# Expert 0's weights behind its gathers, and two experts in split fp32r products

## The chip, the cores and the metric

The kernel runs on one core of a Trainium2 chip. The metric is the device time of one execution in microseconds (us); of several executions the median is taken. A core has a matrix engine (TensorE, PE in the profile; its weight loads are PEld), VectorE (DVE), ScalarE (ACT), GpSimd (POOL) and SyncE (SP), which here only issues DMAs. Each works through its instructions in order. TensorE's granted clock has two levels, 2.4 GHz (1.00 in the rows) and 1.2 GHz (0.50).

## The reference

Three stages, one after the other. q, k and v have 4 batches, 12 heads, 448 positions and 64 values a head.

```python
scores = scale * np.matmul(q, k.transpose(0, 1, 3, 2))      # causal mask, softmax
attn_out = np.matmul(attn, v)                               # 1792 tokens of 768 values
logits = x @ w_gate                                         # 8 experts
# pairs (token, expert) in falling order of logit; a token goes to its best
# expert that has room; an expert takes 224 tokens
for e in range(E):
    h = np.maximum(x[mask] @ w1[e], 0.0)                    # 768 x 1024
    out[mask] = h @ w2[e]                                   # 1024 x 768
gate = 1.0 / (1.0 + np.exp(-(x @ w_gate2)))                 # 768 x 1536
return (gate * (x @ w_val) @ w_out).astype(np.float32)
```

The last stage's weights arrive in 64-bit floating point and are converted in the kernel.

## The kernel before, in words

**Attention** works in 24 units of two heads each (`prep`, `qk`, `exps`, `trans`, `av`). `prep` (L248) transposes q or k on TensorE, takes a high part `hi` in fp32r (a float format that TensorE multiplies in one pass) on ScalarE (L258) and the rest `lo` on VectorE (L270). GpSimd copies the high halves into `st` and `qz` (L263, L265), and SyncE brings the other halves to the opposite partitions by DMA (L267, L273). `qk` (L279) multiplies them, two products a head with 112 weight columns (L290, L291). Ahead of that, GpSimd sets up constants, fills the mask (L237), loads the gate weights `wr` (L240) and splits them into `wg` (L241, L242); `logits` (L373) uses `wg` one unit later.

**Routing** finds the tokens of an expert in a phase (`phase`, L515); phase 0 runs alone between attention and the experts. `search` (L474) finds a threshold in levels: compares on VectorE (L490), counts on TensorE (L495), a step back (L507), a new constant (L501). At the end a table of places `o1` (L608) and an operand `r4` (L601, L602) give, over 14 small products (L612), the token numbers `ids` (L615). SyncE stores them to `idx_d` (L617), 224 numbers of 4 bytes, which only the last stage reads. Two indirect DMAs of GpSimd (`gather`, L739) fetch the 224 token rows of 3 KB each from `x_d`. `xprep` (L744) transposes them (L752). The phases of experts 1 to 7 are spread between the products of the experts (`tick`, `step`): TensorE's order there is that of the program, and its routing products are put in after a count of estimated product times.

**The experts** (`moe`, L758) take one expert after the other, 4 chunks of w1 and 4 of w2, each 768 KB, loaded by SyncE in two halves (`load_chunk` L666, `load_half` L696). Chunks go by turns into buffers `wh` and `wl`, four each, so eight chunks can be ahead. Chunks 2 to 7 are put behind the store of the places of expert 0 in the order of issue (L674); no semaphore holds them. A product `mm` (L713) of an expert is in fp32: 96 products of 128 weight columns and 224 tokens, which the trace shows as 192 matmuls.

**moe2** (L804) is the last stage, in two halves of tokens. Its chunks are converted by `conv_half` and `conv_split` (L65 to L94) into high and low parts (buffers `wh` and `wl` again), and every product is three fp32r products of high and low parts. The first half converts and stores the parts to DRAM, the second reads them back.

A scheduler orders the instructions of all engines but TensorE by simulated times when the kernel is built; `issue_after` adds an order without a wait, `high_priority` moves instructions ahead, `add_manual_dep` adds a dependence that is waited for.

Of the kernel before, what the change touches and what calls it, by code (L numbers as in the profile page):

```python
# [7 lines left out]
F32 = mybir.dt.float32  # L8
# [22 lines left out]
def body(ctx: ExitStack, tc: tile.TileContext, q, k, v, moe_w_gate, moe_w1, moe_w2,  # L31
# [46 lines left out]
    def conv_split(cs, hn, ln):  # L78


        hw, lw = cs[:, :, 1], cs[:, :, 0]
        k3 = cv.tile([128, HC], U32, name="k3")
        nc.scalar.activation(k3, lw, AF.Copy, scale=2.0 ** -29)
        sq = cv.tile([128, HC], F32, name="sq")
# [21 lines left out]
    colp = ct([R, 128], BF, "colp")  # L106
    nc.gpsimd.iota(colp, pattern=[[1, 128]], base=0, channel_multiplier=0, allow_small_or_imprecise_dtypes=True)
# [129 lines left out]
    nc.gpsimd.memset(mask[:, :S - P], 0.0)  # L237
# [3 lines left out]
    nc.gpsimd.tensor_copy(wg[:, :, :E], wr)  # L241
    nc.gpsimd.tensor_tensor(wg[:, :, E:], wr, wg[:, :, :E].bitcast(F32), op=OP.subtract)  # L242
# [171 lines left out]
    for f in [prep(1, 0), prep(1, 1)]:  # L414
        f()
    for s in range(LA):
        qk(*steps[s])
# [49 lines left out]
    fins, after, ist = {}, {}, {}  # L467
# [6 lines left out]
    def search(key, half):  # L474
        base = cst = None
        for lv, (J, st_) in enumerate(LEVELS):
            s_ = st_ * (65536.0 if half == 0 else 1.0)
            thr = JC[half, st_]
            if lv:
                tt = rtile([R, 33], F32, "thr")  # L480
                V.tensor_scalar(tt[:, :J], thr, acc, cst, op0=OP.add, op1=OP.add)
                thr = tt[:, :J]
            ca = rps([R, 128])
            c, a = ca[:E, :64], ca[:, 64:]
            cmps = []
            for hf in range(2):
                ts = slice(hf * T // 2, (hf + 1) * T // 2)
                cmp = rtile([R, T // 2, 64], BF, "cmp", bufs=2)
                with tc.issue_after(after.pop("cmp")) if "cmp" in after else ExitStack():
                    V.tensor_tensor(cmp[:, :, :J], key[:, ts, None].to_broadcast([R, T // 2, J]),  # L490
                                    thr[:, None, :].to_broadcast([R, T // 2, J]), op=OP.is_ge)
# [12 lines left out]
            ge = rtile([E, 64], BF, "ge")  # L504
            V.tensor_scalar(ge[:, :K_], c[:, :K_], rem8, None, op0=OP.is_ge)
            yield Y[3]
            nc.tensor.matmul(a[:, :K_], STEP[half, st_], ge[:, :K_], start=True, stop=True)  # L507
            jk = rtile([R, 64], F32, "jk")
            acc = rtile([R, 1], F32, "acc", bufs=2)
            V.tensor_scalar(jk[:, :K_], a[:, :K_], s_, None, op0=OP.min, op1=OP.add, accum_out=acc)  # L510
        th = rtile([R, 1], F32, "th", bufs=2)
        V.tensor_tensor(th, acc, cst, op=OP.add)
        return th, thr, c

    def phase(ph):  # L515
# [101 lines left out]
        ist[ph] = nc.sync.dma_start(idx_d[ph * CAP:(ph + 1) * CAP].rearrange("(h p) o -> p (h o)", p=P), ids[ph])  # L617
# [48 lines left out]
    def load_chunk():  # L666
        kind, a, c = chunks[stream["next"]]
        if kind in ("w1", "w2") and a not in regs:
            regs[a] = nc.sync.value_load(ei[a][0:1, 0:1], min_val=0, max_val=E - 1)
        if kind in ("w1", "w2"):  # L670
# [25 lines left out]
    def load_half(kind, a, c, n, raw):  # L696
        if kind == "w1":
            src = moe_w1[bass.ds(regs[a], 1), n * 384:(n + 1) * 384, c * 256:(c + 1) * 256]
            nc.sync.dma_start(raw.rearrange("p (c f) -> p c f", c=3),
                              src.rearrange("a (c p) f -> p (a c) f", p=128))  # L700
        else:
# [3 lines left out]
            nc.sync.dma_start(raw.rearrange("p (c f) -> p c f", c=2),  # L705
                              src.rearrange("a (c p) f -> p (a c) f", p=128))
# [28 lines left out]
    def gather(ph):  # L735
        xs = []
        for h in range(2):
            xg = mo.tile([P, DM], F32, name="xg", bufs=2)
            nc.gpsimd.indirect_dma_start(out=xg, out_offset=None, in_=x_d[:],  # L739
                                         in_offset=bass.IndirectOffsetOnAxis(ap=ids[ph][:, h:h + 1], axis=0))  # L740
            xs.append(xg)
        XE[ph] = xs

    def xprep(ph):  # L744
        xs = XE[ph]
        xx = mo.tile([128, KD, CAP], F32, name="xx", bufs=2)
        for dp in range(3):
# [5 lines left out]
            nc.scalar.activation(xx[:, 2 * dp:2 * dp + 2], w.rearrange("p a h q -> p a (h q)"), AF.Copy)  # L753
        XE[ph] = xx
# [3 lines left out]
    def moe(ph, nxt):  # L758
        xx = XE[ph]
        hs_ = []  # L760
        for c in range(4):
            w = use(("w1", ph, c)).rearrange("p (c f) -> p c f", c=KD)
            if c % 2 == 0:
                hs_.append(mp.tile([128, 4, CAP], F32, name="hx", bufs=3))
            g = ps.tile([128, 512], F32, name="g", bufs=7)
            for f in range(2):
                for d in range(KD):
                    mm(g[:, f * CAP:(f + 1) * CAP], w[:, d, f * 128:(f + 1) * 128], xx[:, d], d == 0, d == KD - 1)
            hx = hs_[c // 2][:, 2 * (c % 2):2 * (c % 2) + 2]
            nc.scalar.activation(hx, g[:, :2 * CAP].rearrange("p (a t) -> p a t", a=2), AF.Relu)  # L770
# [8 lines left out]
        for dp in range(0, KD, 2):  # L779
# [4 lines left out]
            for f0, f1 in ((0, 6), (6, 8)) if dp == 0 else ((0, 8),):  # L784
                for n in range(2):
                    d = dp + n
                    for f in range(f0, f1):
                        a = ws[2 * (d // 3) + f // 4].rearrange("p (c f) -> p c f", c=4)
                        mm(yo[n], a[:, f % 4, (d % 3) * 128:(d % 3) * 128 + 128], hs_[f // 4][:, f % 4], f == 0, f == 7)
# [116 lines left out]
```

## Time and profile before

| | us |
|---|---|
| median of 3 runs | 1171.52 (1170.42 to 1171.89) |
| the profiled execution | 1172.35 |
| its span, from the first to the last instruction | 1170.6 |
| busy in it: PE, DVE, ACT, POOL | 1121.1, 595.0, 368.1, 118.3 |
| mean granted TensorE clock | 0.98 |

All rows come from the profiled execution; times in them are us from the start of its span. Durations of groups are means in ns where they stand after a comma. A bracket at the end of a timeline row is the idle time of the engine ahead of it and what ended it. "To landing" is the time from the issue of a DMA to the semaphore that tells of its end.

### The profile page before, as it was taken

The page shows a single profiled execution, that of the slowest core. Times are in us where ns is not written, and L with a number is a line of the kernel's source. Part 1 is how long each engine was busy: PE and PEld are TensorE (multiplying, and loading weights), DVE is VectorE, ACT ScalarE, POOL GpSimd, SP SyncE. Part 2 cuts the span into 40 slices and gives each one's busy share as a digit, 9 for nine tenths or more (in the row PEclk, how much of TensorE's full clock was granted, in tenths as well). Part 3 has the DMA queues.
Part 4 walks back from the last instruction along what each step waited for, and adds up shares of the span by engine and source line. Part 5 has one row for each costly group of instructions (what it writes and reads, how often), then busy time and mean ns, then how long its engine had stood idle before and what let it go on. Part 6 is the DMA issues. An engine that isn't in the chain of part 4 may idle for free.

```text
span 1170.6 us, 19295 instructions
## 1 busy us (share of the span) xinstructions
PE 1121.1 (96%) x7317; PEld 1047.0 (89%) x7317; DVE 595.0 (51%) x1855; ACT 368.1 (31%) x723; POOL 118.3 (10%) x231
## 2 busy tenths in 40 slices
PE   6999999962999999999999999999999999999997
PEld 5999999951888898899999999999999999999997
DVE  5777777763554455450028668688625103223223
ACT  4767676730011110121126544443312220100100
POOL 6333333200000000000000000000002000000002
PEclk9999999975999999999999999999999999999999
DMA  8555656336477665767569555565335333333302
GB/s 167 119 143 146 151 139 157 75 101 184 147 151 184 129 166 156 176 189 198 186 214 326 211 208 218 197 227 203 139 108 203 108 108 108 108 108 109 109 1 95
DMA packets 159581, 180.62 MB, mean 154 GB/s; under 512 B 74864, under 2 KB 140416, under 8 KB 159488
## 3 DMA queue, kind: packets, MB, share of 16 engines
q1 hardware_dynamic: 156064, 168.11, 47.1%
q0 software_dynamic: 2496, 11.04, 4.7%
q8 instruction: 58, 0.95, 0.3%
q14 instruction: 35, 0.29, 0.1%
q10 hardware_dynamic: 928, 0.23, 0.1%
HBM read 129.01 MB, written 39.33 MB: 144 GB/s over the span
## 4 chain that ended last, share of the span: by engine, by line
PE 93%; DMA 3%; DVE 2%; POOL 1%; issue 1%; POOLq 0%; SPq 0%
PE g L714 70%; PE o L343 8%; PE w L323 4%; PE s L290 2%; PE s L291 2%; DMA xg<-x_d,ids 2%; PE r L495 2%; PE w L252 1%; PE g L752 1%; PE w L381 1%; PE w L364 1%; PE r L507 0%; DMA wl<-in_moe_w_dram 0%; DMA wr<-in_moe_w_gate_dram 0%; POOL qz L233 0%
## 5 line engine op out<-in xcount | busy, mean ns | idle before, releaser
L714 PE MATMUL g<-x2h,wh 128*128 128x448 f32 x576 | 212.1, 368 | 0.0
L714 PE MATMUL g<-x2h,wl 128*128 128x448 f32 x576 | 212.0, 368 | 0.0
L714 PE MATMUL g<-x2l,wh 128*128 128x448 f32 x576 | 212.0, 368 | 0.0
L714 PE MATMUL g<-wh,hx 128*128 128x384 f32 x672 | 172.5, 334 | 0.0
L823 DVE TENSOR_TENSOR g<-g,gv 128x448 f32<-128x448 f32 x48 | 30.3, 632 | 219.2 <-PE g L714 219.1
L714 PEld LDWEIGHTS g<-wh,hx 128*128 128x128 f32 x672 | 121.5, 188 | 0.2
L714 PEld LDWEIGHTS g<-x2h,wl 128*128 128x128 f32 x576 | 108.1, 188 | 10.8
L714 PEld LDWEIGHTS g<-x2h,wh 128*128 128x128 f32 x576 | 108.1, 188 | 10.8
L714 PEld LDWEIGHTS g<-x2l,wh 128*128 128x128 f32 x576 | 108.1, 188 | 10.6
L714 PE MATMUL g<-wl,hx 128*128 128x384 f32 x336 | 112.2, 334 | 0.0
L343 PE MATMUL o<-vt,pt 112*112 112x65 f32 x960 | 106.4, 258 | 0.1
L343 PEld LDWEIGHTS o<-vt,pt 112*112 112x112 f32 x960 | 101.9, 178 | 0.3 <-DVE pt L312 0.3
L847 DVE TENSOR_TENSOR acc<-g,acc 128x384 f32<-128x384 f32 x140 | 75.8, 555 | 38.3 <-PE g L714 38.2
L301 ACT ACTIVATE sm<-sm,mn 112x112 f32<-112x112 f32 (+1 forms) x192 | 90.3, 522 | 6.5 <-DVE mn L293 6.5
L293 DVE CUSTOM_DVE_ANT_0 sm<-s,mask 112x112 f32<-112x112 f32 (+1 forms) x192 | 78.3, 444 | 24.3 <-PE s L291 24.1
L714 PE MATMUL g<-hx,wh 128*128 128x224 f32 x384 | 87.3, 361 | 0.0
L714 PE MATMUL g<-xx,wh 128*128 128x224 f32 x384 | 83.7, 364 | 0.0
L714 PE MATMUL g<-hx,wl 128*128 128x224 f32 x384 | 83.0, 356 | 0.0
L94 DVE TENSOR_TENSOR wl<-ca,wh 128x768 fp32r<-128x768 f32 x36 | 33.3, 955 | 91.9 <-PE g L714 81.9
L714 PE MATMUL g<-xx,wl 128*128 128x224 f32 x384 | 79.8, 357 | 0.0
L820 ACT ACTIVATE gv<-g 128x448 f32<-128x448 f32 x48 | 26.0, 542 | 168.0 <-PE g L714 168.0
L714 PEld LDWEIGHTS g<-xx,wh 128*128 128x128 f32 x384 | 71.5, 193 | 1.2
(188 smaller groups left out, 1621.5 us busy)
## 6 DMA issues: line engine op xcount, KB each, us to landing
wh<-in_moe_w_dram SPq DMA_DIRECT2D x64, 384.0 KB, 4.8
wl<-in_moe_w_dram SPq DMA_DIRECT2D x64, 384.0 KB, 5.6
wsc<-wh SPq DMA_DIRECT2D x18, 768.0 KB, 3.3
wsc<-wl SPq DMA_DIRECT2D x18, 768.0 KB, 4.4
wl<-wsc SPq DMA_DIRECT2D x36, 384.0 KB, 4.8
wh<-wsc SPq DMA_DIRECT2D x36, 384.0 KB, 4.4
cs<-in_moe_w_gate_dram SPq DMA_DIRECT2D x12, 768.0 KB, 5.0
cs<-in_moe_w_val_dram SPq DMA_DIRECT2D x12, 768.0 KB, 6.2
```

The source lines that it names most:

```text
L94: nc.vector.tensor_tensor(ln, w_, hn.bitcast(F32), op=OP.subtract)
L290: nc.tensor.matmul(ss[j], qq[:, j, qs], kh[:, j, :w], start=True, stop=False)
L291: nc.tensor.matmul(ss[j], QZ[u % NZ][:, j, qs], kl[:, :w], start=False, stop=True)
L293: nc.vector.tensor_tensor_reduce(sm[:, j, :w], ss[j], mask[:, S - w:], op0=OP.add, op1=OP.min, scale=1.0, scalar=3.0e38, accum_out=mn[:, j ...
L301: nc.scalar.activation(sm[:, j, :w], sm[:, j, :w], AF.Exp, bias=mn[:, j:j + 1], scale=-1.0)
L323: nc.tensor.transpose(w[:P, n, :], sm[:, j, c * P:(c + 1) * P], ident[:P, :P])
L343: nc.tensor.matmul(o[:, n, j, :], pt[:, j * (i + 1) + c, :], vt[:, j, c, :], start=c == 0, stop=c == i)
L495: nc.tensor.matmul(c[:, :J], oha[:, tt_, :], cmps[2 * tt_ // T][:, tt_ % (T // 2), :J], start=tt_ == 0, stop=tt_ == T - 1)
L714: nc.tensor.matmul(o, a, b, start=first, stop=last_)
L820: nc.scalar.activation(gv, pg[:, :448], AF.Sigmoid)
L823: nc.vector.tensor_tensor(pv[:, :448], pv[:, :448], gv, op=OP.mult)
L847: nc.vector.tensor_tensor(ac, po[:, :384], ac, op=OP.add)
```

## The change

- The split of the gate weights moves on GpSimd from ahead of the load of unit 1 to behind the casts of units 0 and 1; part of the mask is filled by VectorE in place of GpSimd.
- In `search`, the constant of a level is issued behind the compares of that level. `r4` is made ahead of the table `o1`; the table has 112 columns that are computed and 16 that are set to zero once.
- Chunks 2 to 7 (expert 0's later weights) wait for both gathers of expert 0, by a dependence that is waited for.
- Experts 6 and 7 compute each product as three fp32r products (high x high, high x low, low x high). Their weights are loaded into `raw` buffers (four halves); ScalarE makes the high part and VectorE the low part. Such a chunk takes a `wh` and a `wl` buffer, so four can be ahead. Token rows and hidden values get low parts too. `k3` and `sq` of the conversion have one buffer each in place of two.

```diff
+        k3 = cv.tile([128, HC], U32, name="k3", bufs=1)
+        sq = cv.tile([128, HC], F32, name="sq", bufs=1)
...
-    colp = ct([R, 128], BF, "colp")
+    colp = ct([R, P], BF, "colp")
+    o1 = ct([R, T, 128], BF, "o1")
...
-    nc.gpsimd.memset(mask[:, :S - P], 0.0)
+    nc.vector.memset(mask[:, :S - P], 0.0)
     nc.gpsimd.dma_start(wr, moe_w_gate.rearrange("(c p) e -> p c e", p=128))
-    nc.gpsimd.tensor_copy(wg[:, :, :E], wr)
-    nc.gpsimd.tensor_tensor(wg[:, :, E:], wr, wg[:, :, :E].bitcast(F32), op=OP.subtract)
...
     for f in [prep(1, 0), prep(1, 1)]:
         f()
+    nc.gpsimd.tensor_copy(wg[:, :, :E], wr)
+    nc.gpsimd.tensor_tensor(wg[:, :, E:], wr, wg[:, :, :E].bitcast(F32), op=OP.subtract)
+    nc.gpsimd.memset(o1[:, :, P:], 0.0)
...
-                V.tensor_scalar(nc_, acc, cst, -s_, op0=OP.add, op1=OP.add)
+                with tc.issue_after(cmpi.ins):
+                    V.tensor_scalar(nc_, acc, cst, -s_, op0=OP.add, op1=OP.add)
...
-        V.tensor_tensor(r4[:, :, 0:2], tp, r4[:, :, 2:4], op=OP.subtract)
+        r4i = V.tensor_tensor(r4[:, :, 0:2], tp, r4[:, :, 2:4], op=OP.subtract).ins
-        o1 = rtile([R, T, 128], BF, "o1")
-            ones[ph] = V.tensor_tensor(o1[:, ts], pm[:, ts, None].to_broadcast([R, T // 2, 128]),
-                                       colp[:, None, :].to_broadcast([R, T // 2, 128]), op=OP.is_equal)
+            with tc.issue_after(r4i):
+                ones[ph] = V.tensor_tensor(o1[:, ts, :P], pm[:, ts, None].to_broadcast([R, T // 2, P]),
+                                           colp[:, None, :].to_broadcast([R, T // 2, P]), op=OP.is_equal)
...
+    SPLIT = (E - 2, E - 1)
...
+        if kind in ("w1", "w2") and a in SPLIT:
+            wh_, wl_ = (mp.tile([128, CH], F32R, name=n, bufs=WB) for n in ("wh", "wl"))
+            for n in range(2):
+                cc = slice(n * 768, (n + 1) * 768)
+                raw = mo.tile([128, 768], F32, name="raw", bufs=4)
+                load_half(kind, a, c, n, raw)
+                nc.scalar.activation(wh_[:, cc], raw, AF.Copy)
+                nc.vector.tensor_tensor(wl_[:, cc], raw, wh_[:, cc].bitcast(F32), op=OP.subtract)
+            W[chunks[stream["next"]]] = (wh_, wl_)
...
-                with tc.issue_after(ist[0].ins) if 2 <= stream["next"] < 8 else ExitStack():
-                    load_half(kind, a, c, n, raw)
+                d_ = load_half(kind, a, c, n, raw)
+                if 2 <= stream["next"] < 8:
+                    for g_ in g0:
+                        tc.add_manual_dep(d_, g_.name, mybir.DependencyInfo(mybir.DependencyClass.Sync,
+                                                                            mybir.DependencyReason.DATA),
+                                          reason="the rows first")
...
+            if ph == 0:
+                g0.append(g_.ins)
...
     def xprep(ph):
+        sp = ph in SPLIT
+        xx = mo.tile([128, KD, CAP], F32R if sp else F32, name="xx", bufs=2)
+        xl = mo.tile([128, KD, CAP], F32R, name="xl", bufs=1) if sp else None
...
+            nc.scalar.activation(xx[:, dd_], wf, AF.Copy)
+            if sp:
+                nc.vector.tensor_tensor(xl[:, dd_], wf, xx[:, dd_].bitcast(F32), op=OP.subtract)
...
     def moe(ph, nxt):
+        def prod(o, w, x, first, last_):
+            if sp:
+                (wh_, wl_), (xh_, xl_) = w, x
+                mm(o, wh_, xh_, first, False)
+                mm(o, wh_, xl_, False, False)
+                mm(o, wl_, xh_, False, last_)
+            else:
+                mm(o, w, x, first, last_)
...
+            nc.scalar.activation(hx[0] if sp else hx, gg, AF.Relu)
+            if sp:
+                nc.vector.scalar_tensor_tensor(hx[1], gg, 0.0, hx[0].bitcast(F32), op0=OP.max, op1=OP.subtract)
```

## Rows read from the trace of the kernel before

**Rows 1.** The page: the chain that ended last, by engine.
```profile
PE 93%; DMA 3%; DVE 2%; POOL 1%; issue 1%; POOLq 0%; SPq 0%
```
**Rows 2.** Stretches: us, busy PE PEld DVE ACT POOL, clock, DMA share, GB/s.
```profile
280.00:282.00 2.00, 0.00 (x0) 0.00 (x0) 0.00 (x0) 0.00 (x0) 0.00 (x0) 0.50 0.66 70
...
280.00:290.00 10.00, 1.28 (x6) 0.96 (x7) 0.00 (x0) 0.00 (x0) 0.00 (x0) 0.50 0.97 234
...
530.00:560.00 30.00, 30.00 (x166) 29.95 (x165) 0.00 (x0) 4.97 (x12) 1.86 (x2) 1.00 0.70 179
```
**Rows 3.** Timeline of the start: us, duration, engine, line, operation.
```profile
8.36 1.19 SPq L273 DMA_DIRECT2D st<-lo  x2
...
9.97 0.22 POOL L241 CAST wg<-wr 128x48 fp32r<-128x48 f32 x1 [2.09 <-DMA wr<-in_moe_w_gate_dram]
...
13.35 0.43 PE L290 MATMUL s<-st,st 128*112 128x112 f32 x1 [3.94 <-POOL st L263]
...
14.34 1.19 SPq L273 DMA_DIRECT2D st<-lo  x2
...
19.26 0.28 PE L290 MATMUL s<-st,st 128*112 128x112 f32 x1
```
**Rows 4.** DMA issues at 8.36 and at 14.34: KB each, us to landing.
```profile
st<-lo SPq DMA_DIRECT2D x1, 112.0 KB, 2.8
...
st<-lo SPq DMA_DIRECT2D x1, 112.0 KB, 3.7
```
**Rows 5.** Timeline of phase 0, VectorE.
```profile
252.62 0.21 DVE L501 TENSOR_SCALAR cst<-acc,cst 128x1 f32<-128x1 f32 x1
...
269.15 2.08 DVE L608 TENSOR_TENSOR o<-pm,colp 128x896 bf16<-128x896 bf16 x2
```
**Rows 6.** Timeline: the stores of the places of experts 0 and 1, expert 0's transposes.
```profile
272.57 0.33 SPq L617 DMA_DIRECT2D idx_d<-ids  x1
...
289.33 2.13 PE L752 MATMUL g<-ident,xg 112*128 112x112 f32 x10 [3.13 <-DMA xg<-x_d,ids]
...
320.74 0.33 SPq L617 DMA_DIRECT2D idx_d<-ids  x1
```
**Rows 7.** Pieces of the chain: start us, us, what.
```profile
274.99 14.29 DMA xg<-x_d,ids
...
322.70 12.52 DMA xg<-x_d,ids
...
555.83 36.34 PE g L714 x192
```
**Rows 8.** DMA to landing, us: issues 272.5 to 275.1, 320.7 to 322.8, 554 to 557.3.
```profile
wh<-in_moe_w_dram SPq DMA_DIRECT2D x2, 384.0 KB, 9.9
...
idx_d<-ids SPq DMA_DIRECT2D x1, 0.9 KB, 8.5
...
idx_d<-ids SPq DMA_DIRECT2D x1, 0.9 KB, 11.5
...
xg<-x_d,ids POOLq DMA_INDIRECT x2, 5.2
```
**Rows 9.** Timeline of TensorE: fp32r score products, 112 and 224 columns.
```profile
105.98 0.26 PE L290 MATMUL s<-st,st 128*112 128x112 f32 x1
106.08 0.26 PE L291 MATMUL s<-lo,qz 128*112 128x112 f32 x1
...
108.12 0.27 PE L290 MATMUL s<-st,st 128*112 128x224 f32 x1
108.22 0.28 PE L291 MATMUL s<-lo,qz 128*112 128x224 f32 x1
```
**Rows 10.** A copy (ns min/median/max), a subtract, weight loads from 560 to 600.
```profile
L93 ACT ACTIVATE wh<-ca x36: 828/837/852, 601.4 to 840.3; 128x768 fp32r<-128x768 f32 x36
...
L94 DVE TENSOR_TENSOR wl<-ca,wh 128x768 fp32r<-128x768 f32 x36 | 33.3, 955 | 91.9 <-PE g L714 81.9 <-ACT wh L93 8.6 <-issue 1.1
...
wh<-in_moe_w_dram SPq DMA_DIRECT2D x8, 384.0 KB, 3.8
```

More of the change, by code (lines that the diff above doesn't have):

```diff
@@ L466, in body @@
     HO = 5000
-    fins, after, ist = {}, {}, {}
+    fins, after, g0 = {}, {}, []
     have = []
@@ L616, in phase @@
         have.append(ph)
-        ist[ph] = nc.sync.dma_start(idx_d[ph * CAP:(ph + 1) * CAP].rearrange("(h p) o -> p (h o)", p=P), ids[ph])
+        nc.sync.dma_start(idx_d[ph * CAP:(ph + 1) * CAP].rearrange("(h p) o -> p (h o)", p=P), ids[ph])
         if not last:
@@ L669, in load_chunk @@
             regs[a] = nc.sync.value_load(ei[a][0:1, 0:1], min_val=0, max_val=E - 1)
+        if kind in ("w1", "w2") and a in SPLIT:
[7 more added lines that the diff above has]
+            W[chunks[stream["next"]]] = (wh_, wl_)
+            stream["next"] += 1
+            return
         if kind in ("w1", "w2"):
@@ L698, in load_half @@
             src = moe_w1[bass.ds(regs[a], 1), n * 384:(n + 1) * 384, c * 256:(c + 1) * 256]
-            nc.sync.dma_start(raw.rearrange("p (c f) -> p c f", c=3),
-                              src.rearrange("a (c p) f -> p (a c) f", p=128))
+            d_ = nc.sync.dma_start(raw.rearrange("p (c f) -> p c f", c=3),
+                                   src.rearrange("a (c p) f -> p (a c) f", p=128))
         else:
@@ L704, in load_half @@
             src = moe_w2[bass.ds(regs[a], 1), r0:r0 + 256, dh * 384:(dh + 1) * 384]
-            nc.sync.dma_start(raw.rearrange("p (c f) -> p c f", c=2),
-                              src.rearrange("a (c p) f -> p (a c) f", p=128))
+            d_ = nc.sync.dma_start(raw.rearrange("p (c f) -> p c f", c=2),
+                                   src.rearrange("a (c p) f -> p (a c) f", p=128))
+        return d_.ins
     def use(key):
@@ L752, in xprep @@
                     nc.tensor.transpose(w[:, dd, h, :], xs[h][:, d * 128:(d + 1) * 128], ident[:P, :P])
-            nc.scalar.activation(xx[:, 2 * dp:2 * dp + 2], w.rearrange("p a h q -> p a (h q)"), AF.Copy)
-        XE[ph] = xx
+            wf = w.rearrange("p a h q -> p a (h q)")
+            dd_ = slice(2 * dp, 2 * dp + 2)
+            nc.scalar.activation(xx[:, dd_], wf, AF.Copy)
+            if sp:
+                nc.vector.tensor_tensor(xl[:, dd_], wf, xx[:, dd_].bitcast(F32), op=OP.subtract)
+        XE[ph] = (xx, xl) if sp else xx
         gat["x"] = ph + 1
@@ L760, in moe, with each @@
         hs_ = []
+        sp = ph in SPLIT
+        def prod(o, w, x, first, last_):
[6 more added lines that the diff above has]
+                mm(o, w, x, first, last_)
+        def each(t, f):
+            return tuple(f(x) for x in t) if sp else f(t)
         for c in range(4):
-            w = use(("w1", ph, c)).rearrange("p (c f) -> p c f", c=KD)
+            w = each(use(("w1", ph, c)), lambda t: t.rearrange("p (c f) -> p c f", c=KD))
             if c % 2 == 0:
-                hs_.append(mp.tile([128, 4, CAP], F32, name="hx", bufs=3))
+                if sp:
+                    h2 = mp.tile([128, 2, 4, CAP], F32R, name="hx", bufs=3)
+                    hs_.append((h2[:, 0], h2[:, 1]))
+                else:
+                    hs_.append(mp.tile([128, 4, CAP], F32, name="hx", bufs=3))
             g = ps.tile([128, 512], F32, name="g", bufs=7)
@@ L767, in moe @@
                 for d in range(KD):
-                    mm(g[:, f * CAP:(f + 1) * CAP], w[:, d, f * 128:(f + 1) * 128], xx[:, d], d == 0, d == KD - 1)
-            hx = hs_[c // 2][:, 2 * (c % 2):2 * (c % 2) + 2]
-            nc.scalar.activation(hx, g[:, :2 * CAP].rearrange("p (a t) -> p a t", a=2), AF.Relu)
+                    prod(g[:, f * CAP:(f + 1) * CAP], each(w, lambda t: t[:, d, f * 128:(f + 1) * 128]),
+                         each(xx, lambda t: t[:, d]), d == 0, d == KD - 1)
+            hx = each(hs_[c // 2], lambda t: t[:, 2 * (c % 2):2 * (c % 2) + 2])
+            gg = g[:, :2 * CAP].rearrange("p (a t) -> p a t", a=2)
+            nc.scalar.activation(hx[0] if sp else hx, gg, AF.Relu)
+            if sp:
+                nc.vector.scalar_tensor_tensor(hx[1], gg, 0.0, hx[0].bitcast(F32), op0=OP.max, op1=OP.subtract)
         blk, half = divmod(ph, 2)
@@ L787, in moe @@
                     for f in range(f0, f1):
-                        a = ws[2 * (d // 3) + f // 4].rearrange("p (c f) -> p c f", c=4)
-                        mm(yo[n], a[:, f % 4, (d % 3) * 128:(d % 3) * 128 + 128], hs_[f // 4][:, f % 4], f == 0, f == 7)
+                        a = each(ws[2 * (d // 3) + f // 4], lambda t: t.rearrange("p (c f) -> p c f", c=4)
+                                 [:, f % 4, (d % 3) * 128:(d % 3) * 128 + 128])
+                        prod(yo[n], a, each(hs_[f // 4], lambda t: t[:, f % 4]), f == 0, f == 7)
                     if nxt is not None and f1 == 8 and d == 4:
```

9 lines of the change are left out of this document (3 added, 6 removed).

## The prediction

> **What bounds the kernel now.** I read the chain of waits first: TensorE holds 93% of the span, DMA 3% [rows 1]. So a change pays where it shortens TensorE's own work, or where TensorE stands still. The table of stretches says where that is [rows 2]: the experts (530 to 560 us) run TensorE without a hole, while from 280 to 290 us it works 1.28 us of 10, at a granted clock of 0.50 (the 1.2 GHz level), with VectorE, ScalarE and GpSimd at zero and the DMA engines at 0.97. That hole is the hand-over from attention to expert 0. A third place is the start, where the first score product at 13.35 us has stood 3.94 us behind GpSimd [rows 3]. The three costly edits go to these three places: start, hand-over, and the pure TensorE time of experts 6 and 7.
>
> **The start.** GpSimd stands 2.09 us for the gate weights, casts them, and only then casts the query halves that the first product reads [rows 3]. The change moves both gate casts behind the casts of units 0 and 1, and the mask memset to VectorE, which has no work there that TensorE awaits. GpSimd is then early enough, and the next one late is the swapped low half: issued at 8.36 us, landing 2.8 us later [rows 3, 4], at 11.2. The first product could gain 13.35 - 11.2 = 2.2 us. But unit 1's low halves are issued by SyncE, which does not move, in the pair that starts at 14.34, and land 3.7 us later, at 18.0, the second about 0.6 us after it; the product that reads them starts at 19.26 now [rows 3, 4]. So 1.2 us remain before the first head and about 0.8 before the second. I take **1.0 us**; ends 0 (the loads of unit 2 hold it) and 2.2. The gate weights are first used a whole unit later, so their own move costs nothing.
>
> **The chain before expert 0.** Here VectorE and TensorE take turns and every instruction counts. The constant of a search level (0.21 us, row of L501) goes behind the compares; there are four such levels in a phase, ends 0 and 0.84 us, I take 0.5, because neighbours on VectorE overlap a little. The place table has 112 columns in place of 128: its 2.08 us [rows 5] shrink by an eighth, 0.26 us. Together 0.76 us. Making the small operand first moves its instruction and adds none. In phases 1 to 7 all of this lies beside TensorE work and is worth nothing; the memset of the padding runs once, on GpSimd, under attention.
>
> **The gathers.** TensorE's transposes wait until 289.33 us [rows 6]; the second gather was issued at 274.99 and took 14.29 us [rows 7]. Two things are in its way. One is the weights: SyncE loads six more chunks of expert 0 behind the store of the places, which is what the change forbids. The other is that store itself: 0.9 KB issued at 272.57 us takes 8.5 us to land [rows 6, 8], until 281.1, and in that time all DMA engines together move 70 GB/s [rows 2], with weights queued. It stays where it is, since the gathers follow it by a microsecond and the held weights come after both on SyncE. For what is left without weights I use expert 1: its store is issued at 320.74 and lands 11.5 us later, at 332.2, its second gather at 322.70 + 12.52 = 335.2 [rows 6, 7, 8], so 3.0 us behind the store, in a time with few weights under way. Expert 0 then: 281.1 - 0.76 + 3.0 = 283.3, against 289.28 now: **6.0 us**, the chain's 0.76 in it. Ends: with a store as slow as expert 1's, 286.3 (3.0 us); with no store stall, the last pair of gathers, which lands in 5.2 us [rows 8]: 275.0 - 0.76 + 5.2 = 279.4 (9.9 us). I take the first store's own 8.5 us, the nearest row.
>
> The Trainium skill's page "DMA: Bandwidth & Descriptors" (section "Specifications") says that transfers under 512 B are done as read-modify-write; the trace agrees as far as it goes, with 8.5 us for 0.9 KB in pieces of 4 bytes, but shows no store by itself.
>
> The wait holds SyncE: behind it stand chunks 2 to 7, then expert 1's index and loads. Chunk 2 is needed after two chunks of 24 passes, 2 x 24 x 36.34/192 = 9.1 us after the first product, which itself follows the gather by 2.1 us of transposes [rows 6, 7]. A weight half lands in 3.8 us undisturbed and in 9.9 us in the worst stretch [rows 8, 10], so it is in time in both cases. Cost zero; if that cover went, each microsecond late would be one on the path.
>
> **Experts 6 and 7.** An expert takes 192 passes in 36.34 us [rows 7], 0.189 us each: two passes for each of 96 fp32 products. The change makes three fp32r products of each: 2 x 96 x 3 = 576 for the two, against 72.7 us. fp32r with a 224-column operand runs in attention: starts 0.10 us apart, and 0.10 as well with 112 columns [rows 9], so the 112-column weights, not the operand, set the pace there. For 128 weight columns that scales to 0.114. I take 0.110, near the scaled end: 63.4 us, a gain of **9.3 us**; ends 0.100 (57.6 us, gain 15.1) and 0.114 (65.7, gain 7.0).
>
> The Trainium skill's page "TensorE: Matmul & The Clock Gate" (section "LDWEIGHTS") gives columns / 1.2 ns for a weight load, 106.7 ns here; by that estimate the two experts would take 61.4 us and the gain would be 11.3.
>
> Each of the 32 weight halves now also needs a ScalarE copy (0.84 us) and a VectorE subtract (0.955) [rows 10]: 27 and 31 us in some 63, on engines that show 5.0 and 0.0 us of 30 in this stretch [rows 2]. TensorE hides them. The raw buffer holds four halves, two chunks; a round takes 3.8 + 0.84 + 0.955 = 5.6 us, 2.8 us a chunk, against 63.4/16 = 4.0 us of products. The look-ahead shrinks from eight chunks to four, still two rounds. moe2's first chunk gets its buffers when the first half of expert 7's second product is done, 72 products or 7.9 us before its end, and needs two copies and two subtracts. Cost zero, up to 3 us if the conversions come late. The single k3 and sq buffers only order ScalarE behind VectorE under the experts, for nothing.
>
> **Sum.** 1.0 + 6.0 + 9.3 = 16.3 us. The profiled execution took 1172.35 us (span 1170.6), 0.83 over the median of the runs; it would come to 1156.0, and the median of 1171.52 to **1155.2 us**.
>
> **Rivals.** *Only the weights held the gathers*: the slow DMA there is the queue of chunks, the store rides along. For it: DMA share 0.97 from 280 to 290. Against: 70 GB/s is not a full queue. The gathers land like the last pair, 9.9 us gained: 1151.3. The Trainium skill's same DMA page (section "Issuing engines are not separate DMA queues") has all issuers share the same 16 engines, which would make the weights the whole cause. 14%.
>
> *The store is the whole cause*, or the wait counts a gather's issue and not its landing, so that the change doesn't hold the weights: gain 0.76 plus the other two, 1160.4. For it: the store's 11.5 us at expert 1. 10%.
>
> *The split doesn't pay*: an fp32r product needs 0.126 us, what a third of an fp32 product costs now, from a pause between products that attention's short bursts hide: 1164.5. 7%.
>
> *Slower: the raw ring starves TensorE.* Place: experts 6 and 7. Two chunks a round, landing + 1.8 us. It decides when the experts need 72.7 + 7.0 + 2.3 (the bound below) = 82.0 us, 5.1 a chunk, a landing of 8.5 us. At the 9.9 us of the gather stretch [rows 8] a chunk takes 5.85 us, 16 of them 93.6: 20.9 lost, 7.0 gained elsewhere, 1185.4. For it: the handshake over SyncE, ScalarE and VectorE is new and in order. Against: 3.8 us over a whole expert [rows 10]. 6%.
>
> **Chances.** The forecast has 58%, with a range of its own from 1149 to 1161; 5% are left for a changed order of instructions that eats the gain. About 0.2%, 2.3 us, is what a measurement can tell from no change. Faster: 58 + 14 + 10 + 7 = 89%; same 4%; slower 7%. The low end, 1147, holds the weights-only rival and part of the quick pace of 0.100; the high end, 1165, holds the rivals up to the split that doesn't pay, as well as a late hand-over to moe2. The starving ring stays outside.
>
> **What would show it.** The first score product near 11 us and unit 1's near 18; the store still some 8 us in landing and the second gather within 3 us of it; chunk 2's load issued only after that landing, with TensorE never waiting for it; products of experts 6 and 7 0.11 us apart without idle time, an expert near 32 us in place of 36.3; moe2 unchanged in length. Wrong is the prediction if TensorE shows waits for wh or wl in the split experts, if the gathers land much before the store, or if products there lie 0.126 us or more apart.

## The result, and the profile after

The changed kernel takes **1157.6 us** (median of 4 runs, 1156.9 to 1158.6) against 1171.7 of the kernel before beside it: a ratio of 0.988, 95% interval 0.987 to 0.990. The forecast was 1155.2 in a range from 1147 to 1165. The profiled execution took 1157.51 us (span 1155.3), 14.8 less than the one before.

The page of the changed kernel, the chain that ended last by engine:

```profile
PE 94%; DMA 3%; DVE 2%; issue 1%; POOL 0%; SPq 0%; POOLq 0%; ACT 0%; DVEq 0%
```

TensorE's share went from 93 to 94% [rows 1], GpSimd's from 1 to 0. The three stretches of [rows 2], the last one moved to where the split experts are now (columns as there):

```profile
280.00:282.00 2.00, 0.00 (x0) 0.00 (x0) 0.00 (x0) 0.00 (x0) 0.00 (x0) 0.50 0.56 135
280.00:290.00 10.00, 7.40 (x43) 6.07 (x43) 1.58 (x8) 1.63 (x3) 0.00 (x0) 0.63 0.63 193
560.00:590.00 30.00, 30.00 (x273) 30.00 (x272) 15.91 (x20) 15.63 (x27) 0.00 (x0) 1.00 0.59 184
```

From 280 to 290 us TensorE now works 7.40 us where it worked 1.28. In the split experts it still has no hole, and VectorE and ScalarE are half busy where they were nearly idle: that is the new work, and it is hidden.

The timeline of the changed kernel (us, duration, engine, line, operation, idle before and its releaser) at the start:

```profile
10.97 0.41 PE L289 MATMUL s<-st,st 128*112 128x112 f32 x1 [1.65 <-DMA st<-lo]
...
14.34 1.18 SPq L272 DMA_DIRECT2D st<-lo  x2
...
18.29 0.28 PE L289 MATMUL s<-st,st 128*112 128x112 f32 x1 [1.92 <-DMA st<-lo]
```

The first score product comes 2.4 us earlier than in [rows 3], and waits for the swapped low half where it waited for GpSimd. Unit 1's low halves are issued at 14.34 as before, so its first product gains only 1.0 us.

The same timeline at the hand-over:

```profile
269.25 0.34 PE L615 MATMUL r<-r,o 128*128 128x4 bf16 x7 [2.50 <-DVE o L611]
...
270.97 0.33 SPq L620 DMA_DIRECT2D idx_d<-ids  x1
...
283.21 2.13 PE L777 MATMUL g<-ident,xg 112*128 112x112 f32 x10 [0.26 <-DMA xg<-x_d,ids]
285.13 1.73 PE L735 MATMUL g<-xx,wh 128*128 128x224 f32 x4
...
283.31 1.57 SPq L719 DMA_DIRECT2D wh<-in_moe_w_dram  x2
```

And its DMA issues from 270.9 to 273.8, with us to landing, and the piece of its chain (start, us, what):

```profile
idx_d<-ids SPq DMA_DIRECT2D x1, 0.9 KB, 9.9
```
```profile
273.69 9.47 DMA xg<-x_d,ids
```

The last transposes start at 283.21 in place of 289.33 [rows 6], and chunk 2's weights are issued at 283.31, after the gather's landing at 283.16: the wait does what it says. The first expert product comes at 285.13, 6.1 us earlier than in the kernel before:

```profile
291.25 1.73 PE L714 MATMUL g<-xx,wh 128*128 128x224 f32 x4
```

But the hole is still there: the gather takes 9.47 us, and the store ahead of it 9.9, with no weights issued behind it. (The last halves of chunk 1, issued from 268.19, still move until about 274 us.)

Products in expert 6, from the timeline of the changed kernel:

```profile
570.38 0.39 PE L735 MATMUL g<-hx,wh 128*128 128x224 f32 x2
570.60 0.27 PE L735 MATMUL g<-hx,wl 128*128 128x224 f32 x1
570.71 0.39 PE L735 MATMUL g<-hx,wh 128*128 128x224 f32 x2
```

Three products start in 0.333 us, 0.111 us each. Expert 6 as a piece of the chain, 36.34 us long before [rows 7]:

```profile
549.41 32.52 PE g L735 x280
```

From the start of expert 6's last transpose to the first product of the last stage 68.6 us pass, where 76.8 passed before: 8.2 us gained.

### The profile page after: what moved, and what is told of

Read it like the earlier page. It is cut to its first block, busy times and chain, and to the rows that moved or that the text cites. A ratio compares the mean times of both kernels' runs of the same rounds, so it can differ in the third digit from the quotient of the medians.

```text
span 1155.3 us, 19791 instructions
## 1 busy us (share of the span) xinstructions
PE 1111.0 (96%) x7509; PEld 1038.1 (90%) x7509; DVE 634.7 (55%) x1902; ACT 394.4 (34%) x755; POOL 118.9 (10%) x231
## 4 chain that ended last, share of the span: by engine, by line
PE 94%; DMA 3%; DVE 2%; issue 1%; POOL 0%; SPq 0%; POOLq 0%; ACT 0%; DVEq 0%
PE g L735 71%; PE o L342 8%; PE w L322 4%; PE s L289 2%; PE s L290 2%; DMA xg<-x_d,ids 2%; PE w L251 2%; PE r L497 2%; PE g L777 1%; PE w L380 1%; PE w L363 1%; DMA st<-lo 1%; PE r L510 0%; DMA qt<-in_q_dram 0%; DVE cmp L492 0%
## 5 line engine op out<-in xcount | busy, mean ns | idle before, releaser
L735 PEld LDWEIGHTS g<-x2h,wl 128*128 128x128 f32 x576 | 108.1, 188 | 10.7
L735 PEld LDWEIGHTS g<-x2h,wh 128*128 128x128 f32 x576 | 108.1, 188 | 10.5
L735 PE MATMUL g<-hx,wh 128*128 128x224 f32 x480 | 99.5, 328 | 0.0
L292 DVE CUSTOM_DVE_ANT_0 sm<-s,mask 112x112 f32<-112x112 f32 (+1 forms) x192 | 78.5, 445 | 22.7 <-PE s L290 22.5
L735 PE MATMUL g<-xx,wh 128*128 128x224 f32 x384 | 90.9, 344 | 0.0
L735 PE MATMUL g<-hx,wl 128*128 128x224 f32 x384 | 89.3, 336 | 0.0
L735 PE MATMUL g<-xx,wl 128*128 128x224 f32 x384 | 87.4, 338 | 0.0
L872 ACT ACTIVATE gv<-g 128x448 f32<-128x448 f32 x48 | 26.1, 544 | 169.0 <-PE g L735 168.9
L735 PEld LDWEIGHTS g<-hx,wh 128*128 128x128 f32 x480 | 80.8, 191 | 1.2
L735 PEld LDWEIGHTS g<-hx,wl 128*128 128x128 f32 x384 | 72.0, 190 | 0.6
```

What stands on the lines that cost most here:

```text
L292: nc.vector.tensor_tensor_reduce(sm[:, j, :w], ss[j], mask[:, S - w:], op0=OP.add, op1=OP.min, scale=1.0, scalar=3.0e38, accum_out=mn[:, j ...
L735: nc.tensor.matmul(o, a, b, start=first, stop=last_)
L872: nc.scalar.activation(gv, pg[:, :448], AF.Sigmoid)
```

## The experiments

Kernels were timed in groups, each beside the kernel before on one chip, whose median went from 1171.6 to 1173.7 us between groups. Across groups the ratios compare, not the medians. The code changes below are shown shortened.

| kernel | median, us | ratio to before (95%) |
|---|---|---|
| the change | 1157.6 | 0.988 (0.987 to 0.990) |
| no split | 1164.7 | 0.994 (0.993 to 0.996) |
| no hold | 1164.4 | 0.994 (0.993 to 0.996) |
| store late, hold | 1152.0 | 0.985 (0.983 to 0.987) |
| store late, no hold | 1156.2 | 0.987 (0.986 to 0.989) |
| start and chain back | 1161.6 | single run |
| half operand | 1160.2 | single run |
| raw ring of two | 1175.3 | single run |
| store late, 7 experts split | 1181.6 | 1.008 (1.005 to 1.011) |
| the same, subtract on GpSimd | 1230.9 | 1.050 (1.047 to 1.053) |
| store late, 3 experts split | 1162.9 | 0.992 (0.990 to 0.993) |
| one store for all | 1152.0 | 0.982 (0.980 to 0.983) |
| **one store, 3 experts split** | **1149.3** | **0.979 (0.978 to 0.981)** |

### The hand-over: store and weights, each with and without the other

**No hold.** The wait on the gathers is taken out, and the old order behind the store is back:

```
-    add_manual_dep(d_, gathers of expert 0)
+    with tc.issue_after(ist[0].ins): load_half(kind, a, c, n, raw)
```

> The changed kernel without the wait: chunks 2 to 7 are ordered behind the store only, as before the change. The store of the places stays ahead of the gathers. Theory (both the store and the weights delay the gathers, the weights by 4 to 5 us of it): the gathers land 4 us later, the first expert product at 289.1 in place of 285.1, time 1161.6. Rival 1 (the store is the whole cause, the wait gains nothing): 285.1 and 1157.6. Rival 2 (the earlier end of the routing chain alone moved the gathers): within 1 us of the changed kernel.

**Store late, hold.** Expert 0's store goes behind its last weight load:

```
-    nc.sync.dma_start(idx_d[expert 0], ids[0])        # as soon as the ids are there
+    if stream["next"] == 8:
+        with tc.issue_after(last load of chunk 7): store(0)
```

> The changed kernel with expert 0's store of the places issued behind its last weight load, so that nothing but the two gathers is under way when the ids are ready. Theory (what is left of the hole is the store): the second gather, issued at 273.7, lands like the last pair of the kernel, 3.8 to 5.2 us later, at 278 to 279 in place of 283.2; first expert product near 280.5, time 1153. Rival (the gathers of this stretch are slow by themselves, from rows just written or many small descriptors): landing unchanged at 283, time 1157.6. A second rival says that the store now stalls chunks of expert 1 or the gathers of expert 1: then TensorE waits for wh, wl or xg show up after 300 us and the gain is smaller than the landing's.

**Store late, no hold.** As the last, and the six chunks wait for the ids instead of the gathers:

```
-    for g_ in g0:
+    for g_ in [fins[0].ins]:
```

> As the late store, but the weight loads of chunks 2 to 7 wait for the ids only and not for the gathers, so that weights and gathers run together without the store. Theory (store and weights delay the gathers each by its own means: the weights by sharing the engines, 0.69 MB of rows against 4.7 MB of weights): second gather lands 2 to 4 us after the late-store kernel's, at 280 to 283, time 1155 to 1157. Rival 1 (weights alone cost nothing, they only lengthen the store): as the late store, 278 to 279, 1153. Rival 2 (the weights alone make the whole hole): landing near 288, as in the kernel before, time 1162.

The second gather's piece in the chain of each (start, us, what): no hold, store late with hold, store late without.

```profile
275.14 15.16 DMA xg<-x_d,ids
```
```profile
273.64 4.29 DMA xg<-x_d,ids
```
```profile
273.33 8.96 DMA xg<-x_d,ids
```

With the change's 9.47 these make a table of two by two. The last number of each cell is the time from the first place-table product to the first expert product.

| | weights beside the gathers | weights held |
|---|---|---|
| store ahead | 15.16 us, 21.6 (kernel before: 14.29, 19.9) | 9.47 us, 15.9 |
| store late | 8.96 us, 15.4 | 4.29 us, 10.7 |

The weights cost 5.7 us with the store and 4.7 without it; the store costs 6.2 and 5.2. The two nearly add: neither is the whole cause, and neither works through the other. Both single-cause rivals fall, here and in the prediction. Each cell is one execution; in four more with the store ahead and the weights held the gather took 9.4 to 10.5 us, so a difference of 1 us between these sums is not told from scatter.

The kernel without the hold needs 1.7 us more in this stretch than the kernel before. Half of that is the measure: in the changed kernels the place-table products begin with half of the table ready, 0.56 us further ahead of the ids, and the first gather's instruction takes 0.3 us longer (see the chain, below). The other 0.9 is the gather's own. The theory for it had 4 us; its first expert product came at 292.27, 7.1 us behind the change's, of which 1.5 come from the start. Its profiled execution (1164.8 us; the six runs took 1161.5 to 1168.5) carries those too (last section).

In the kernel with the late store and the hold TensorE waits for no weights and no rows after 300 us, so the store that was moved holds up nothing there: the second rival falls.

**One store for all.** The eight stores go away altogether:

```
-    nc.sync.dma_start(idx_d[ph], ids[ph])             # 224 pieces of 4 bytes, per expert
+    V.tensor_copy(idsf[:, 2 * ph:2 * ph + 2], ids[ph])
...
+    nc.tensor.transpose(w, idsf, ident[:P, :P])       # once, beside expert 6
+    V.tensor_copy(idst, w)
+    nc.gpsimd.dma_start(idx_d as 16 rows of 112, idst)
```

> The changed kernel without any of the eight stores of places in pieces of 4 bytes: the ids of all experts are collected, transposed once on TensorE beside expert 6 and stored once, in 16 pieces of 448 bytes. Theory (the store alone is what is left of the hole at expert 0, and the stores alone made the gathers of experts 1 to 6 take 8 to 13 us): gathers of experts 1 to 6 land in 4 to 6 us after their issue, the first expert product comes at 279.9 as with the late store, and, because all of the later gathers were hidden, the time is that of the late store, 1152. Rival 1 (the gathers of the middle experts are slow from the weights beside them, 4 to 6 us of it, as the 2 by 2 of store and hold showed for expert 0): they still take 8 to 10 us. Rival 2 (the one store is as slow as eight, since its pieces too are under 512 bytes): a landing of 8 us or more and a stretch of low DMA throughput near 580 us.

Its DMA issues, with us to landing: the gathers of expert 4 (from 424 us) and the one store (577). Behind them the same gathers in the changed kernel (from 429.8).

```profile
xg<-x_d,ids POOLq DMA_INDIRECT x2, 5.2
...
idx_d<-idst POOLq DMA_DIRECT2D x1, 7.0 KB, 1.6
```
```profile
xg<-x_d,ids POOLq DMA_INDIRECT x2, 12.1
idx_d<-ids SPq DMA_DIRECT2D x1, 0.9 KB, 6.8
```

The first expert product comes at 280.23, as with the late store (279.90), and the gathers in the middle fall from 12.1 to 5.2 us. So the stores alone made those slow; the weights beside them cost little there. Those gathers were hidden, and the time is that of the late store: the medians are equal, the spans 1150.2 and 1149.4. (The ratios differ by 0.003; one of the late store's five runs, at 1158.8, lies 5 us above the rest.)

### The split

**No split.** `SPLIT = ()`, all else as changed.

> The changed kernel with experts 6 and 7 back in fp32 products; start, chain and hand-over stay as changed. Theory (the split alone gave what the trace shows for experts 6 and 7, 3.8 + 4.35 = 8.2 us, and nothing else in the kernel hangs on it): 1157.6 + 8.2 = 1165.8 us, both experts 36.3 us again, first expert product still at 285.1. Rival (the look-ahead halved by the split gives part of its gain back, elsewhere than in the two experts, for instance at the hand-over to the last stage): the loss is more than 8.2, and the last stage, whose length went down by 0.7 us with the change, changes too.

The two experts take 76.8 us again, to 0.01 us what they took before, against 68.6: the split's share is 8.2 us in the trace. The spans differ by 7.5 us (1162.8 against 1155.3), since this execution reached expert 6 0.9 us earlier; the medians differ by 7.1. The last stage is 531.3 us long here and 531.1 in the changed kernel (531.8 before), so the split doesn't shorten it, and its 0.7 us are no part of the mechanism.

**Half operand.** What sets the 0.111 us?

```
-    mm(o, wh_, xl_, False, False)
+    mm(o[:, :CAP // 2], wh_, xl_[:, :CAP // 2], False, False)
```

> The changed kernel in which one of the three products of each triple in experts 6 and 7 (weights' high part by operand's low part) covers only the first 112 of the 224 operand columns; that part of the low product is left out for the other tokens. Theory (an fp32r product there takes as long as its 128 weight columns take to load): all products stay 0.111 us apart, time 1157.6. Rival (the 224 operand columns set the pace): the 192 half products take half, 192 x 0.055 = 10.6 us less, 1147. In between (the two share it): a half product of about 0.098 us, 2.5 us less, 1155.

Its products in expert 6, as shown above for the change:

```profile
572.07 0.34 PE L735 MATMUL g<-hx,wh 128*128 128x224 f32 x2
572.24 0.33 PE L735 MATMUL g<-hx,wl 128*128 128x224 f32 x1
572.40 0.33 PE L735 MATMUL g<-hx,wh 128*128 128x224 f32 x2
```

The pair with the half operand takes 0.17 us in place of 0.22, and the product behind it takes the rest: a triple still needs 0.333 us, and the two experts 68.6. So the operand's columns don't set the pace. That the weight loads do is argued, not shown: PEld is busy all 30 us from 560 to 590 in the change (above), and attention's 112 weight columns go faster, at 0.10 us [rows 9]; in the experts the weight columns were not varied. What the time has over the change lies ahead of the edit: expert 6 begins 2.7 us later, 2.0 of them from the start (last section). The Trainium skill's page "TensorE: Matmul & The Clock Gate" (section "LDWEIGHTS") gives 106.7 ns for 128 weight columns; the 111 ns measured are 4% above it.

**Raw ring of two.** `bufs=4` becomes `bufs=2` for the raw halves.

> The changed kernel with two raw buffers in place of four: one chunk a round instead of two, and a round is landing 3.7 + copy 0.84 + subtract 0.955 = 5.5 us against 4.0 us of products a chunk. Theory (the raw ring decides whether TensorE starves, and four buffers have margin because the landing is 3.7 us): 16 chunks take 88 us against 64 us of products and some 16 us of look-ahead (four chunks), TensorE waits about 8 us for wh or wl in experts 6 and 7, time 1166. Rival (the four converted chunks ahead cover even this, the starving case was never near): no waits, 1157.6.

The longest waits of its TensorE from 500 to 640 us (in total, times, longest), and ScalarE's timeline ahead of the longest:

```profile
PE g L735 <- ACT hx L819: 7.2, 3, 5.0
PE g L735 <- ACT xx L780: 1.5, 1, 1.5
```
```profile
541.59 0.84 ACT L681 ACTIVATE wh<-raw 128x768 fp32r<-128x768 f32 x1 [1.57 <-DMA raw<-in_moe_w_dram]
542.34 0.53 ACT L819 ACTIVATE hx<-g 128x448 f32<-128x448 f32 x1
```

The starving case is real: experts 5 to 7 take 17.0 us longer than in the change, twice what I expected, 7.2 of them already in expert 5, beside which expert 6's first chunks are converted. It does not show as a wait for weights: ScalarE takes its work in order, so the Relu that TensorE needs stands behind a copy that waits for a raw half. The pauses also let the granted clock fall: from 540 to 547 us it was 0.51. With four buffers nothing of this appears.

### Start and chain

**Start and chain back.** Gate casts and mask memset ahead again, the old order of the chain and 128 place-table columns:

> The changed kernel with the two small edits undone, each read at its own place: the gate casts and the mask memset back ahead of the operand casts on GpSimd, and the routing chain in its old order with the place table 128 columns wide. Theory (the start and the chain each keep what they gain there): first score product at 13.3 in place of 10.97 and unit 1's first at 19.3 in place of 18.29; end of attention 1.2 us later; from the first compare product to the first place-table product 22.55 us in place of 21.56; first expert product 2.1 us later than the changed kernel's, time 1159.7. Rival (the next wait, the loads of unit 2 or the low halves, takes the start's gain back before the end of attention): attention ends where it does in the changed kernel and only the chain's 1 us is lost, 1158.6.

Its timeline at three places:

```profile
13.44 0.44 PE L291 MATMUL s<-st,st 128*112 128x112 f32 x1 [4.05 <-POOL st L264]
...
20.17 0.29 PE L291 MATMUL s<-st,st 128*112 128x112 f32 x1
...
271.81 0.54 PE L614 MATMUL r<-r,o 128*128 128x4 bf16 x14 [3.57 <-DVE r L604]
```

The first product is late by 2.5 us, unit 1's by 1.9, and the end of attention (the first routing product on TensorE) by 1.6 (249.33 against 247.69). The start keeps what it gains, 1.2 to 1.6 us, and the rival that a next wait takes it back falls. The chain keeps little. From the end of attention the first place-table product comes 0.9 us earlier in the change (21.6 against 22.5), but the ids only 0.4 (23.1 against 23.5), and the second gather's issue 0.1 (26.0 against 26.1). The first expert product is late by 2.55 us (287.68): 1.7 at that issue, and the rest is the gather itself, 10.31 us here against 9.47, which lies within the scatter (above). That the sum is near what the theory had, 2.1, is luck. The span is 4.4 us over the change's; 1.3 of the rest lies in the last stage, which neither edit touches.

### More experts split

If an expert saves 4.1 us, why only two? Three kernels with the late store asked that. `SPLIT` is `tuple(range(1, E))` in the first two, `(E - 3, E - 2, E - 1)` in the third, and the second moves one operation:

```
-    nc.vector.tensor_tensor(wl_[:, cc], raw, ...)
+    nc.gpsimd.tensor_tensor(wl_[:, cc], raw, ...)
```

> Late store, hold, and experts 1 to 7 in split products. Theory (each expert so converted saves the 4.1 us that the two of the changed kernel save, since VectorE and ScalarE have room: 16.2 and 3.0 us busy of 30 in the stretch after 300 us): 1152 - 5 x 4.1 = 1131.5. Rival 1 (the routing chain of the next expert queues behind the subtracts on VectorE): TensorE waits for cmp, ge or o in experts 1 to 5, some us an expert, 1140 to 1150. Rival 2 (a store of places stalls the loads for 7 to 12 us and four chunks of look-ahead do not cover it): TensorE waits for wh or wl in experts 1 to 5, up to 5 us an expert, 1155.

> As the kernel with experts 1 to 7 split and the late store (1181.6 us), but the subtract that makes the low half of the weights runs on GpSimd, which has nothing else there but the gathers. Theory (that kernel lost its time because VectorE, in order, held the routing chain behind subtracts that waited for ScalarE's copies and these for TensorE to free a buffer): the waits of TensorE for o, ge and cmp (38 us in all) fall to a few us, the clock stays at 2.4 GHz, and the time goes toward 1131 to 1140. Rival 1 (GpSimd takes 1.24 ns a column in its casts; with two operands up to twice that, 1.9 us a half and 3.8 us a chunk, as long as the products of a chunk): TensorE waits for wl, 1150 to 1175. Rival 2 (the loads themselves, stalled by the stores, are late): TensorE waits for wh after each store, time above 1150 and no better than the other.

> Late store, hold, and experts 5, 6 and 7 in split products, with the subtracts on VectorE as in the change. Theory (a split expert saves 4.1 us where no routing phase runs beside it; only the last phase's end lies in expert 5): 1152 - 4.1 = 1148, with at most 2 us of new waits of TensorE for o or ge around 510 to 525 us. Rival (one phase beside it is enough to cost what the split saves, since with experts 1 to 5 split each lost about 10 us): 1152 to 1158, with waits for o, ge or cmp near the start of expert 5.

Seven experts split lost some 27 us against the late store (by the ratios). TensorE's waits, the first three lines of that kernel, then of the one with the subtract on GpSimd, and that one's GpSimd and VectorE lines (the group lines as in [rows 10]):

```profile
PE r L618 <- DVE o L614: 15.3, 9, 5.3
PE r L510 <- DVE ge L508: 11.8, 14, 3.8
PE r L497 <- DVE cmp L492: 11.0, 11, 1.6
```
```profile
PE r L618 <- DVE o L614: 25.0, 10, 6.9
PE r L497 <- DVE cmp L492: 21.1, 18, 2.4
...
L689 POOL TENSOR_TENSOR wl<-raw,wh 128x768 fp32r<-128x768 f32 x84 | 157.3, 1896 | 165.4 <-ACT wh L688 134.5 <-DMA raw<-in_moe_w_dram 30.4 <-issue 0.4
...
L492 DVE TENSOR_TENSOR cmp<-key,thr 128x224 bf16<-128x224 f32 (+1 forms) x20 | 14.7, 779 | 0.3
```

TensorE waits for the routing chain on VectorE, as rival 1 said: after 300 us these three come to 12.3, 9.3 and 3.0 us with VectorE's subtract, and the changed kernel has none of them there. The granted clock falls in the gaps (mean 0.95 from 300 to 620 us). On GpSimd it got worse, against my theory: a subtract takes 1.90 us there, twice VectorE's 0.955 [rows 10], and VectorE's own compares slow from 395 ns in the changed kernel to 779 beside it.

With three experts split the cause can be seen in a single place. TensorE's and VectorE's timeline of that kernel:

```profile
485.14 0.20 PE L510 MATMUL r<-ge,sv 8*128 8x64 bf16 x1 [7.02 <-DVE ge L508]
...
483.05 1.85 DVE L689 TENSOR_TENSOR wl<-raw,wh 128x768 fp32r<-128x768 f32 x2 [7.34 <-DMA raw<-in_moe_w_dram]
484.82 0.27 DVE L508 TENSOR_SCALAR ge<-r,rem 8x64 bf16<-8x64 f32 x1
```

VectorE's next routing step (ge) stands behind two subtracts, these behind a raw half that lands late, and TensorE behind ge: 7.0 us, and the clock at 0.50 from 480 to 490. Expert 4 takes 10.9 us longer by it, and expert 5 gains 0.9 where 4.1 were to be won; by the ratios the kernel loses 8 us against the late store.

**One store, three experts split** takes the suspected root away, the store of 4-byte pieces that was issued 3 us ahead of those raw halves:

> One store for all ids, hold, and experts 5, 6 and 7 in split products. Theory (with eight stores, the split of expert 5 lost 10 us because a store stalled a weight half, VectorE's subtract waited 7.3 us for it and the routing step behind it made TensorE wait 7.0 us and the clock fall for 10 us; without the stores this is gone): no wait of TensorE for ge above 2 us, no fall of the clock, 1152 - 4.1 = 1148. Rival (the subtract waits for ScalarE's copy and a free buffer in any case, so the routing step is held with or without stores): a wait of several us near 480 us remains and the time is 1155 to 1163.

TensorE's waits for ge in the whole of that kernel:

```profile
PE r L512 <- DVE ge L510: 2.8, 8, 0.4
```

The 7.0 us are gone, the clock doesn't fall, and the kernel takes 1149.3 us, 0.979 of the kernel before: the best of all, 2.6 us better than with two experts split. 4.1 were expected; expert 5 itself takes 3.8 us less, and expert 4, where its first chunks are converted beside the routing, 2.0 more. So the split gives 1.8, and the rest is scatter (the last stage alone is 1.2 us shorter). The stall at 478 us thus came from the store. That the seven-expert kernels would be cured the same way was not tried.

## Why the prediction came out as it did

**Start** (1.0 forecast). Right in its mechanism: low halves at 10.97 (11.2 said) and 18.29 (18.0 said). The end of attention came 1.16 us earlier, 1.6 by the run that undid it.

**Chain** (0.76). Too large, and wrong in its larger part. One search level on VectorE, the ids and the first gather, of the kernel before and then of the changed one:

```profile
252.41 0.30 DVE L481 TENSOR_SCALAR thr<-jc,acc,cst 128x32 f32<-128x32 f32 x1
252.75 0.69 DVE L490 TENSOR_TENSOR cmp<-hs,thr 128x224 bf16<-128x224 f32 x2
...
272.38 0.16 DVE L615 SCALAR_TENSOR_TENSOR ids<-c 112x2 int32<-112x2 f32 x1
...
273.60 1.08 POOL L739 DMA_INDIRECT xg<-x_d,ids  x1 [47.95 <-DMA wl<-in_moe_w_dram]
```
```profile
251.33 0.30 DVE L483 TENSOR_SCALAR thr<-jc,acc,cst 128x32 f32<-128x32 f32 x1
251.66 0.69 DVE L492 TENSOR_TENSOR cmp<-hs,thr 128x224 bf16<-128x224 f32 x2
...
270.79 0.15 DVE L618 SCALAR_TENSOR_TENSOR ids<-c 112x2 int32<-112x2 f32 x1
...
272.01 1.38 POOL L760 DMA_INDIRECT xg<-x_d,ids  x1 [47.50 <-DVE be L185]
```

From the threshold to the compare 0.34 us pass with the constant between them [rows 5] and 0.33 without it. So the constants gave nothing where I took 0.5: I had them overlap a little, and they overlapped wholly. The narrower table gave its term, 1.85 us in place of 2.08. The first place-table product stands 0.99 us earlier behind the end of attention (248.85 before, 247.69 now), but it needs half of the table only, and the products of the other half wait 0.54 us more. The ids come 0.43 us earlier, and the second gather's issue 0.14, since the first gather's instruction on GpSimd takes 1.38 us in place of 1.08. Why it does is open.

**Gathers** (6.0 with the chain). The step "store landing plus 3.0" held: the gather landed 2.3 us behind the store. The term that was mis-sized is the store: 9.9 us in place of 8.5, though no weights were issued behind it. I took "the first store's own" as the nearest row; expert 1's 11.5 us, the end I set aside, was as near. Nor was expert 1's stretch one with few weights: from 320 to 322 us the engines moved 349 GB/s there. The hand-over gained 5.0 us, 4.8 in the gather and 0.14 in the chain. That the gather came within 0.4 us of its forecast is in part luck, since the store's 1.4 us too little and the 0.7 too much behind it go against each other.

**Waiting SyncE** (zero). Right: no wait of TensorE for chunks 2 to 7.

**Split** (9.3). Mechanism right, size off: 0.112 us a product for 0.110. Scaling the 112-column pace by weight columns gave 0.114, the taken value was a guess between, and 576 products turn 0.002 us into 1.1. Conversions were hidden, as said; the raw ring did not starve, but with half the buffers it does, so the 6% stood for a real mechanism.

**Rivals.** *Only the weights* gave 1151.3, by landing the gathers in 5.2 us: the late-store kernel lands them in 4.3 and takes 1152.0, so its number was right for a kernel that also moves the store. *Store is the whole cause* falls with the kernel without the hold, and *the split doesn't pay* with 0.111 us a product. The page's rule that issuers share the same engines (the Trainium skill, "DMA: Bandwidth & Descriptors", section "Issuing engines are not separate DMA queues") agrees with half of the hole: 4.7 us when weights run beside the gathers. That it would make the weights the whole cause was my reading, and the store's half shows it wrong.

In sum, at the first expert product 7.0 were forecast and 6.1 came (start 1.16, chain 0.14, gather 4.82), in the split experts 9.3 and 8.2. The last stage gave 0.7 us that I did not forecast and that no run ties to the change: in kernels that leave it as changed it lasts 531.1 to 532.5 us.

## What to carry to other kernels

A store of a few hundred 4-byte pieces is not small: look at what else the DMA engines moved until it landed, and keep it away from a transfer that the critical path waits for, or turn it into a few long rows. When two suspects share a stall, run all four combinations; here each explained half. And before work is put on an idle engine, ask what waits in order behind it: an operand conversion that waits for a load holds every later step on that engine.

## What the runs showed of the hardware beyond that

- **Piece size.** One store of 7.0 KB in 16 pieces of 448 bytes landed in 1.6 us; 0.9 KB in 224 pieces of 4 bytes took 6.8 to 9.9 in the changed kernel, and from 276 to 280 us, while the first such store was under way, all DMA engines together moved 57 to 63 GB/s. The Trainium skill's rule on transfers under 512 B ("DMA: Bandwidth & Descriptors", section "Specifications") covers both alike, so that bound alone does not tell them apart. The one store also goes by GpSimd's queue and at another place; whether the number of the pieces or their size counts is not shown.
- **GpSimd beside VectorE.** With subtracts on GpSimd, VectorE's compares of 395 ns took 779 on average where they read `key` and 504 where they read `hs`; those of 448 columns stayed at 622 and 614.
- **A dip of the clock at the start.** In the kernels without the hold and with the half operand, stretches of the start show a lower clock. Of the first, and then of the changed kernel (us, busy PE, PEld, DVE, ACT, POOL, clock, DMA share, GB/s):

```profile
17.00:20.00 3.00, 1.89 (x19) 1.68 (x18) 1.93 (x9) 1.15 (x3) 0.85 (x2) 1.00 1.12 200
20.00:23.40 3.40, 3.40 (x21) 3.40 (x20) 2.27 (x9) 1.51 (x5) 1.04 (x2) 0.50 0.49 95
```
```profile
17.00:20.00 3.00, 1.53 (x14) 1.46 (x15) 1.21 (x6) 0.86 (x2) 0.79 (x2) 1.00 0.90 199
20.00:23.40 3.40, 3.40 (x36) 3.40 (x36) 2.17 (x9) 2.57 (x8) 1.23 (x3) 1.00 0.66 138
```

The clock rose, and fell back to the 1.2 GHz level for some 3.4 us after a stretch in which TensorE was busy 1.89 of 3.00 us (the half operand: 2.03 of 2.90). In the changed kernel it was busy less, 1.53 of 3.00, and the clock stayed, so that share alone does not tell why it fell; the cause is open. Attention then ended at 249.25 and 249.71 in place of 247.69. Neither edit touches that stretch, so two runs of one kernel may well differ by 2 us this way, as much as the smaller terms of this forecast; two executions of one kernel were not compared for it.
